# The first search of a token router: four rounds of 32 thresholds, or three rounds that begin with 128

## The chip, the cores and the metric

The kernel runs on one core of one Trainium2 chip. A core has five engines that work side by side, each through its own instructions in their order: TensorE (PE, matrix multiplies), VectorE (DVE), ScalarE (ACT), GpSimd (POOL) and SyncE (SP, which here only issues transfers). The metric is the device time of one execution in microseconds (us), lower is better. Before the change the median of three runs is 596.17 us (596.12 to 596.48).

## The reference

An attention block with pooled keys and values feeds a mixture of experts whose tokens are assigned greedily. What matters here is the assignment:

```python
def _moe_ref(x, w_gate, w1, w2):
    N, D = x.shape                      # 4608 tokens, 512
    E = w_gate.shape[1]                 # 8 experts
    cap = N // E                        # 576 places each
    logits = x @ w_gate
    order = np.argsort(-logits.flatten())
    assigned = -np.ones(N, dtype=np.int64)
    counts = np.zeros(E, dtype=np.int64)
    for idx in order:
        tok, e = (int(idx) // E, int(idx) % E)
        if assigned[tok] >= 0 or counts[e] >= cap:
            continue
        assigned[tok] = e
        counts[e] += 1
    out = np.zeros((N, D), dtype=np.float32)
    for e in range(E):
        mask = assigned == e
        h = np.maximum(x[mask] @ w1[e], 0.0)
        out[mask] = h @ w2[e]
```

Here x is the output of attention (8 batches, 8 heads, 576 positions, head size 64, keys and values averaged over groups of 8), seen as 4608 rows of 512.

## The kernel before

**Attention in 36 tiles.** The 4608 tokens are worked through in 36 tiles of 128, numbered 0 to 35; a tile is also a column of the routing arrays (128 partitions, 36 columns, 8 experts). The loop in `run` (class `Attention`) is a software pipeline. In its step n, TensorE computes the scores of tile n (`st_s`, L230, into the one PSUM buffer `pss`), then transposes the softmax of tile n-1 (`st_e`, L259) and multiplies tile n-2 with the values (`st_av`, L272). VectorE takes the row maximum of the scores (L240, `mx`) and subtracts it (L241, `e`), and then norms tile n-3 (`norm`: reciprocal L284, gate logits L287, and L297 `xt`). Every fourth tile, a reduction (L290, `lg`) writes the logits of four tiles; only the last four tiles do that one by one. Scores of tile n+1 cannot begin before `e` of tile n has emptied `pss`. Since an engine takes its instructions in order, whatever VectorE is given at the end of step n stands in front of the row maximum of tile n+1.

GpSimd sums the keys and values of the next batches over their groups of 8 (`pool_k` L175 to L179, `pool_v` L188 to L198), batch after batch; the last batch is finished in step 29. In two steps of each batch TensorE also prepares its values (`prep_v` L211, `prep_g` L220).

**The first search.** The greedy assignment is done expert by expert: the router looks for the logit value at which the first expert becomes full, gives all tokens above it to their best expert, closes that expert and goes on. The value is found by thresholds. Each token's best logit is turned into a place on a scale (`q`), compared with `J` = 32 levels (`cmp`), and TensorE counts, for each level and expert, the tokens above it, column by column: a matmul with `cmp` as weights and the one-hot best expert `oh` as moving operand (L709). A test finds the levels at which some expert has more than 576 (`over`, L751), a matmul of ones counts these levels and spreads the result to all partitions (L755), and the scale is made finer by 32/1.125 round the level found. This is done four times (`rounds` = 4) in `search_first`.

What can be done before the last logits are there is spread over the steps of attention, by the dictionary handed to `A.run` in the kernel's main function. Its keys are the tile that has just been normed, so key k is worked off at the end of step k+3: the range of all logits of the first 24 columns in three steps (`bounds`, keys 25 to 27), best logit, place and one-hot of columns 0 to 27 (`best`, key 28), comparison of columns 0 to 15 and 16 to 27 (keys 29, 30), the levels themselves (key 31) and finer places (key 32). The columns 28 to 33, 34 and 35 follow in `begin`, between the last pieces of attention in `finish`.

After the search, `close` builds the list of rows of the expert; its number goes to a load of expert weights, the list to GpSimd, which gathers the rows. In between, matmuls that only keep TensorE busy are run (`warm`, L530). Then the expert's matmuls begin (L1210), and the searches of the other experts run beside them.

## Time and profile before

| | |
|---|---|
| median of three runs | 596.17 us |
| the profiled execution's own time | 596.39 us |
| its span, first to last instruction | 594.6 us |
| PE busy, share of the span | 574.0 us, 97% |
| DVE busy | 392.9 us, 66% |
| ACT busy | 305.1 us, 51% |
| POOL busy | 178.6 us, 30% |
| chain that ended last, by engine | PE 83%, issue 7%, DVE 4%, POOL 3%, DMA 1% |

The time of an execution is a little longer than the span, since it includes what lies before the first and after the last instruction. The page divides the span into 40 slices of 14.9 us. TensorE is 90% busy or more in all of them but the first, the last and the one from 134 to 149 us, where it is 50% to 60% busy and its granted clock is 0.6 of full speed. That is the passage from attention to the experts.

### The profile page before, as it was taken

To read this page: it belongs to the slowest core of one execution; us is meant where nothing else is said; L and a number is where in the kernel's file an instruction comes from. 1 tells how busy PE (TensorE), PEld (TensorE's weight loads), DVE (VectorE), ACT (ScalarE), POOL (GpSimd) and SP (SyncE) were. 2 spreads that over 40 slices of the span, in tenths; PEclk is the share of its full clock that TensorE was granted. 3 is DMA by queue.
4 is the path that set the end of the run, shared out by engine and by line. 5 is a ranking of instruction groups with operands and counts; after the bars stand their busy time and mean duration, and the time that the engine had idled before them with its cause. 6 is when DMAs were issued, how large, how long until landed. Compare 5 with 4: busy or idle time off the path is not lost.

```text
span 594.6 us, 11103 instructions
## 1 busy us (share of the span) xinstructions
PE 574.0 (97%) x4061; PEld 509.3 (86%) x4061; DVE 392.9 (66%) x1146; ACT 305.1 (51%) x633; POOL 178.6 (30%) x228
## 2 busy tenths in 40 slices
PE   8999999995999999999999999999999999999993
PEld 5899999993898799779978987997899899889972
DVE  7677887998886788668866876586487346416200
ACT  6444444452551385376665575285549627835210
POOL 1999999200200410330122221112221212210021
PEclk9999999996999999999999999999999999999997
DMA  8999982112540863538438336543743553350010
GB/s 352 420 423 399 424 321 88 74 72 96 181 143 29 255 204 122 144 107 291 98 99 277 105 81 221 168 107 76 265 129 81 189 201 89 89 196 10 2 58 26
DMA packets 63872, 99.83 MB, mean 168 GB/s; under 512 B 34736, under 2 KB 34752, under 8 KB 61120
## 3 DMA queue, kind: packets, MB, share of 16 engines
q1 hardware_dynamic: 52560, 70.66, 34.8%
q0 software_dynamic: 5920, 18.89, 10.0%
q10 hardware_dynamic: 5328, 9.48, 4.3%
q8 instruction: 34, 0.56, 0.4%
q14 instruction: 30, 0.25, 0.1%
HBM read 72.40 MB, written 18.87 MB: 154 GB/s over the span
## 4 chain that ended last, share of the span: by engine, by line
PE 83%; issue 7%; DVE 4%; POOL 3%; DMA 1%; ACT 0%; POOLq 0%; another core or an unknown queue 0%; ACTq 0%; DVEq 0%
PE h L1210 32%; PE h L1246 27%; PE psa L272 6%; PE pss L230 5%; PE h L1251 4%; PE pse L259 2%; PE rt L259 1%; PE rt L530 1%; PE rt L657 1%; DVE e L241 1%; PE rt L220 1%; PE rt L709 1%; DMA out_dram<-yt,rows 1%; PE h L530 1%; PE tp L1183 1%
## 5 line engine op out<-in xcount | busy, mean ns | idle before, releaser
L1246 PE MATMUL h<-w2h,hh 128*128 128x512 f32 x256 | 102.0, 398 | 0.3 <-PEq L1327 0.3
L1246 PE MATMUL h<-w2h,hl 128*128 128x512 f32 x256 | 101.4, 396 | 0.0
L1246 PE MATMUL h<-w2l,hh 128*128 128x512 f32 x256 | 101.0, 395 | 0.0
L1226 POOL DMA_INDIRECT out_dram<-yt,rows x36 | 38.0, 1056 | 193.9 <-ACT yt L1266 167.8
L1215 ACT ACTIVATE hh<-h 128x256 fp32r<-128x256 f32 (+2 forms) x129 | 52.7, 409 | 83.6 <-PE h L1210 83.2
L1210 PE MATMUL h<-xh,w1h 128*128 128x256 f32 (+2 forms) x516 | 93.4, 299 | 0.2 <-ACT xh L1185 0.2
L1210 PE MATMUL h<-xl,w1h 128*128 128x256 f32 (+2 forms) x516 | 91.9, 298 | 0.0
L1210 PE MATMUL h<-xh,w1l 128*128 128x256 f32 (+2 forms) x516 | 90.6, 296 | 0.0
L1210 PEld LDWEIGHTS h<-xh,w1h 128*128 128x128 f32 x516 | 77.0, 190 | 1.2 <-ACT xh L1185 0.5
L1210 PEld LDWEIGHTS h<-xl,w1h 128*128 128x128 f32 x516 | 76.4, 190 | 0.1
L1210 PEld LDWEIGHTS h<-xh,w1l 128*128 128x128 f32 x516 | 76.1, 190 | 0.0
L1114 POOL DMA_INDIRECT xa<-xd,rows x33 | 33.6, 1017 | 137.0 <-ACT xg L1137 40.5
L1220 DVE SCALAR_TENSOR_TENSOR hl<-h,hh 128x256 fp32r<-128x256 f32 (+2 forms) x129 | 56.9, 448 | 21.5 <-ACT hl L1218 10.9
L1266 ACT ACTIVATE yt<-h 128x512 f32<-128x512 f32 x32 | 19.1, 596 | 92.1 <-PE h L1246 78.9
L272 PE MATMUL psa<-vblk,eT 128*128 128x146 f32 (+3 forms) x390 | 59.3, 302 | 0.1
L1246 PEld LDWEIGHTS h<-w2h,hh 128*128 128x128 f32 x256 | 48.3, 189 | 9.3 <-issue 0.7
L1246 PEld LDWEIGHTS h<-w2l,hh 128*128 128x128 f32 x256 | 48.2, 188 | 9.2
L1246 PEld LDWEIGHTS h<-w2h,hl 128*128 128x128 f32 x256 | 48.4, 189 | 8.4
L1163 DVE TENSOR_TENSOR w1l<-raw,w1h 128x512 fp32r<-128x512 f32 x64 | 41.9, 686 | 17.8 <-ACT w1h L1159 17.6
L272 PEld LDWEIGHTS psa<-vblk,eT 128*128 128x128 f32 (+1 forms) x390 | 50.8, 180 | 1.5 <-issue 0.3
L1172 DVE TENSOR_TENSOR w2l<-raw,w2h 128x512 fp32r<-128x512 f32 x64 | 43.3, 682 | 3.3 <-ACT w2h L1169 3.1
L230 PE MATMUL pss<-kblk,rawq 128*128 128x144 f32 (+1 forms) x320 | 43.6, 294 | 0.1
(256 smaller groups left out, 947.1 us busy)
## 6 DMA issues: line engine op xcount, KB each, us to landing
...
```

What stands on the lines that cost most here:

```text
L230: nc.tensor.matmul(ps[cols, j // 2, 144 * (j % 2):144 * (j % 2) + 144], self.q_of(b, j, n, cols.stop - cols.start), self.kblk[b % 4][:, j] ...
L272: self.nc.tensor.matmul(o[h], self.eT[i][:, c, h], self.vblk[b % 4][:, self.BLOCKS[c]:self.BLOCKS[c + 1]], start=(c == cs[0]), stop=(c == ...
L1114: self.nc.gpsimd.indirect_dma_start(out=to[:n], out_offset=None, in_=self.xd, in_offset=bass.IndirectOffsetOnAxis(ap=rows[:n, t:t + 1], ax ...
L1163: self.nc.vector.tensor_tensor(l, raw, h.bitcast(F32), op=OP.subtract)
L1172: self.nc.vector.tensor_tensor(self.w2l[:, i], self.raw2[e][:, i], self.w2h[:, i].bitcast(F32), op=OP.subtract)
L1210: nc.tensor.matmul(ps[:, :m], a[:, j, fs], b[:, j, o], start=(n == 0), stop=(n == 11))
L1215: nc.scalar.activation(hh[:, f, o], ps[:, :m], AF.Relu)
L1220: later(0.65, 0.4, lambda f=f, o=o, m=m, ps=ps: nc.vector.scalar_tensor_tensor(hl[:, f, o], ps[:, :m], 0.0, hh[:, f, o].bitcast(F32), op0= ...
L1226: st = nc.gpsimd.indirect_dma_start(out=rows, out_offset=bass.IndirectOffsetOnAxis(ap=idx, axis=0), in_=y, in_offset=None)
L1246: nc.tensor.matmul(ps, a[:, f, o], b[:, f], start=(f == 0 and k == 0), stop=(f == 7 and k == 2))
L1251: nc.tensor.matmul(ps, self.hl[:, f, 512:], b[:, f], start=(f == 0 and k == 0), stop=(f == 7 and k == 1))
L1266: self.nc.scalar.activation(y, ps, AF.Copy)
```

## The change

The first search does three rounds. The first round has 128 levels, one for each row of the counting matmul's output; the two others have 32 as before. The scale of the first round spans the best logits of the first 16 columns and not all logits of 24. The range is found in seven small steps (`range_of`), on VectorE at keys 16, 17, 18, 21 and 22, with two matmuls that stand in steps 21 and 24 straight behind the scores (`mid`) and whose results ScalarE copies out of PSUM. The comparisons of the first round write 128 levels a column into a buffer of the pool of query tiles (`room`), six columns a step at keys 24 to 27. The last four columns compare logits with levels in 32-bit numbers (`late_tiles`). The product of one-hot and expert weight (`wish`) is done in two parts. The core of the diff (the tiles `thr`, `gz` and `ow` move to a pool that ends with attention; `best`, `top` and the code that is only renamed are left out):

```diff
+            for f in mid.get(n, ()):
+                f()
             e = [lambda g=g: self.st_e(n - 1, g) for g in range(2 if n >= 1 else 0)]
...
-    def bounds(self, wk, cols):
...
+    def range_of(self, i, n=16):
+        nc, wk = self.nc, self.wk
+        lg = self.lg[:, :n].rearrange("p c e -> p (c e)")
+        if i == 0:
...
+            nc.vector.tensor_reduce(self.mm[:, 0:1], lg, axis=AX.X, op=OP.max)
+            nc.vector.tensor_reduce(self.mm[:, 1:2], lg, axis=AX.X, op=OP.min)
+        elif i == 1:
+            nc.vector.tensor_reduce(self.bv[:, :n], self.lg[:, :n], axis=AX.X, op=OP.max)
+            nc.vector.tensor_reduce(self.mm[:, 2:3], self.bv[:, :n], axis=AX.X, op=OP.min)
+            nc.vector.tensor_scalar(self.mm[:, 1:3], self.mm[:, 1:3], -1.0, None, op0=OP.mult)
+        elif i == 2:
+            ps = self.psum()
+            nc.tensor.transpose(ps[:3, :128], self.mm, self.ident)
+            self.m3 = wk.tile([3, 128], F32, name="m3")
+            nc.scalar.activation(self.m3, ps[:3, :128], AF.Copy)
+        elif i == 3:
+            m = wk.tile([3, 1], F32, name="m1")
+            nc.vector.tensor_reduce(m, self.m3, axis=AX.X, op=OP.max)
+            self.d3 = wk.tile([3, 3], F32, name="d3")
+            nc.vector.tensor_scalar(self.d3, self.ident[:3, :3], m, None, op0=OP.mult)
...
+        elif i == 4:
+            ps = self.psum()
+            nc.tensor.matmul(ps[:, :3], self.one3, self.d3, start=True, stop=True)
...
+        elif i == 5:
+            b = self.b
+            nc.vector.tensor_scalar(b[:, 3:5], b[:, 1:3], b[:, 0:1], None, op0=OP.add)
+            nc.vector.scalar_tensor_tensor(self.lo0, b[:, 3:4], -0.125, b[:, 1:2], op0=OP.mult, op1=OP.subtract)
...
+            nc.vector.scalar_tensor_tensor(self.lo1, b[:, 4:5], -0.125, b[:, 2:3], op0=OP.mult, op1=OP.subtract)
+        elif i == 6:
...
+            nc.vector.tensor_scalar(self.steps1, self.shares[:, :3], w, None, op0=OP.mult)
...
+            nc.vector.scalar_tensor_tensor(self.los, self.steps1[:, 0:1], -1.0 - EDGE, self.lo1, op0=OP.mult, op1=OP.add)
...
+    def fresh(self, c0, c1, n=0):
+        nc = self.nc
+        if c1 > n:
+            c = max(c0, n)
+            nc.vector.tensor_reduce(self.bv[:, c:c1], self.lg[:, c:c1], axis=AX.X, op=OP.max)
+        bv = self.bv[:, c0:c1]
+        nc.vector.tensor_scalar(self.q2[:, c0:c1], bv[:, :, None].to_broadcast([128, c1 - c0, 2]), self.lo1, self.scale1,
+                                op0=OP.subtract, op1=OP.mult)
+        nc.vector.tensor_tensor(self.oh[:, c0:c1], self.lg[:, c0:c1], bv[:, :, None].to_broadcast([128, c1 - c0, 8]),
+                                op=OP.is_equal)
+
+    def compare(self, c0, c1):
+        n = c1 - c0
+        if c0 == 0:
+            self.cmp0 = self.room()
+        self.nc.vector.tensor_tensor(self.cmp0[:, c0:c1].rearrange("p c (j t) -> p c j t", t=2),
+                                     self.q2[:, c0:c1, None].to_broadcast([128, n, 64, 2]),
+                                     self.jrow[:, None].to_broadcast([128, n, 128]).rearrange("p c (j t) -> p c j t", t=2),
+                                     op=OP.is_gt)
+
+    def late_tiles(self, c0, c1):
+        nc, n = self.nc, c1 - c0
+        bv = self.bv[:, c0:c1]
+        nc.vector.tensor_reduce(bv, self.lg[:, c0:c1], axis=AX.X, op=OP.max)
+        nc.vector.tensor_tensor(self.cmp0[:, c0:c1], self.thr[:, None].to_broadcast([128, n, 128]),
+                                bv[:, :, None].to_broadcast([128, n, 128]), op=OP.is_lt)
...
-        for k in range(rounds):
-            last = k + 1 == rounds
...
+        ps = self.psum()
+        count(0, NC - 1, lambda c: self.cmp0[:, c])
+        yield 0
+        up = self.bank("pse")[:, :1]
+        self.place(NC - 12, NC)
+        count(NC - 1, NC, lambda c: self.cmp0[:, c])
+        test(0, self.gz)
+        nc.tensor.matmul(up, self.ones, self.gz, start=True, stop=True)
+        for k in (1, 2):
+            q2 = wk.tile([128, NC, 2], F16, name="q2")
+            finer(q2, self.q32[:, :, None].to_broadcast([128, NC, 2]))
+            compare(0, 4, 12, 24, NC)
...
     def begin(self, g):
-        self.best(self.NC - 8, self.NC - 2)
+        NC = self.NC
+        self.compare(NC - 8, NC - 4)
+        self.late_tiles(NC - 4, NC - 2)
+        yield
+        self.late_tiles(NC - 2, NC - 1)
         next(g)
         yield
...
+        A.run(c2, R, lambda: R.consts(A.jp, A.ident), R.more, {
+            16: f(R.range_of, 0), 17: f(R.range_of, 1), 18: f(R.range_of, 3), 20: f(R.before_search, 1),
+            21: f(R.range_of, 5), 22: f(R.range_of, 6) + f(R.before_search, 0), 23: f(R.fresh, 0, 24, 16),
+            24: f(R.compare, 0, 6), 25: f(R.compare, 6, 12), 26: f(R.compare, 12, 18), 27: f(R.compare, 18, 24),
+            28: f(R.fresh, 24, 28), 29: f(R.compare, 24, 28) + f(R.levels), 30: f(R.place, 0, 24) + f(R.wish, 0, 24)
+            + f(wake, nc, R, rwk, moe_w2), 31: f(R.fresh, 28, 32)}, {21: f(R.range_of, 2), 24: f(R.range_of, 4)},
```

Where that puts the instructions, at three places. Line numbers are those of each kernel's own file. First, VectorE in step 26 of attention, before: the subtraction for tile 26, the norm of tile 23 with the reduction of four tiles, and the maximum of tile 27.

```order
L241 TENSOR_TENSOR e<-pss,mx 128x576
L284 RECIPROCAL rinv<-psa 128x8
L287 TENSOR_TENSOR gt_1206<-psa,rinv 128x64
L290 TENSOR_REDUCE lg<-gt_1206 128x32
L297 TENSOR_TENSOR xt<-psa,rinv 128x512
L240 TENSOR_REDUCE mx<-pss 128x8
L241 TENSOR_TENSOR e<-pss,mx 128x576
```

And in the change, from the last instruction of step 25 (`los`, the lowest level) to the maximum of tile 27 (`bv` is the best logit, `q2a` the places, `oh` the one-hot):

```order
L594 SCALAR_TENSOR_TENSOR los<-steps_1325,lo_1290 128x1
L245 TENSOR_REDUCE mx<-pss 128x8
L246 TENSOR_TENSOR e<-pss,mx 128x576
L289 RECIPROCAL rinv<-psa 128x8
L292 TENSOR_TENSOR gt_1224<-psa,rinv 128x64
L295 TENSOR_REDUCE lg<-gt_1224 128x32
L302 TENSOR_TENSOR xt<-psa,rinv 128x512
L617 TENSOR_REDUCE bv_264<-lg 128x8
L619 TENSOR_SCALAR q2a<-bv_264,lo_1290,scale_1327 128x48
L621 TENSOR_TENSOR oh_266<-lg,bv_264 128x192
L245 TENSOR_REDUCE mx<-pss 128x8
```

Three instructions now stand between the norm of tile 23 and the maximum of tile 27. Second, TensorE in step 21, before: scores of tile 21, transposes of tile 20, values of tile 19.

```order
L230 MATMUL pss<-kblk_130,rawq 128x144 x4
L259 MATMUL pse<-ident,e 127x128 x3
L272 MATMUL psa<-vblk_177,eT_172 128x2x73
L272 MATMUL psa<-vblk_177,eT_172 128x3x73
L272 MATMUL psa<-vblk_177,eT_172 128x2x73
```

And in the change (`mm` holds the maximum and the two minima of each partition, written at the end of step 20 by VectorE):

```order
L235 MATMUL pss<-kblk_130,rawq 128x144 x4
L563 MATMUL rt<-ident,mm 3x128
L264 MATMUL pse<-ident,e 127x128 x3
L277 MATMUL psa<-vblk_177,eT_172 128x2x73
L277 MATMUL psa<-vblk_177,eT_172 128x3x73
```

The transpose of `mm` stands in front of the transposes of tile 20. Third, VectorE at the end of attention, from the norm of tile 32 to the reciprocal of tile 34, before:

```order
L297 TENSOR_TENSOR xt<-psa,rinv 128x512
L575 TENSOR_SCALAR q_1681<-bv_262,lo_260,scale 128x28
L284 RECIPROCAL rinv<-psa 128x8
L287 TENSOR_TENSOR gt_1700<-psa,rinv 128x64
L290 TENSOR_REDUCE lg<-gt_1700 128x8
L594 TENSOR_REDUCE bv_262<-lg 128x6
L597 TENSOR_SCALAR q2a<-bv_262,lo_260,scale 128x12
L601 TENSOR_TENSOR oh_264<-lg,bv_262 128x48
L702 TENSOR_TENSOR cmp<-q2a,jrow 128x192
L284 RECIPROCAL rinv<-pss 128x8
```

And in the change (`rawq` is the buffer that holds the comparisons of the first round):

```order
L302 TENSOR_TENSOR xt<-psa,rinv 128x512
L289 RECIPROCAL rinv<-psa 128x8
L292 TENSOR_TENSOR gt_1720<-psa,rinv 128x64
L295 TENSOR_REDUCE lg<-gt_1720 128x8
L629 TENSOR_TENSOR rawq<-q2a,jrow 128x512
L638 TENSOR_REDUCE bv_264<-lg 128x2
L639 TENSOR_TENSOR rawq<-thr,bv_264 128x256
L641 TENSOR_TENSOR oh_266<-lg,bv_264 128x16
L289 RECIPROCAL rinv<-pss 128x8
```

One instruction has gone from behind the norm, and the four of `begin` are others and longer.

## Rows read from the trace of the kernel before

**Rows 1.** The view of stretches for the passage between attention and the experts: stretch and length, then busy time and number of instructions of PE, PEld (TensorE's weight loads), DVE, ACT and POOL, then granted TensorE clock, DMA share and GB/s.

```profile
135.00:143.00 8.00, 4.62 (x115) 3.68 (x114) 6.51 (x36) 2.94 (x13) 0.30 (x4) 0.66 0.20 72
143.00:152.00 9.00, 5.80 (x29) 2.56 (x29) 6.69 (x24) 2.41 (x5) 3.19 (x4) 0.54 0.58 175
```

**Rows 2.** The timeline of the first search from the second round on: start, duration, engine, line, operation, and in brackets idle time before it with what ended it. The tests of the second, third and fourth round, the list of rows, and the first matmul of the first expert.

```profile
137.37 0.17 DVE L751 TENSOR_SCALAR_CACHE_REDUCE over<-rt 32x8 bf16<-32x8 f32 x1
...
139.70 0.17 DVE L751 TENSOR_SCALAR_CACHE_REDUCE over<-rt 32x8 bf16<-32x8 f32 x1
...
142.03 0.17 DVE L751 TENSOR_SCALAR_CACHE_REDUCE over<-rt 32x8 bf16<-32x8 f32 x1
...
147.45 0.17 DVE L850 TENSOR_SCALAR rows<-found 128x5 int32<-128x5 int16 x1
...
152.55 0.67 PE L1210 MATMUL h<-xh,w1h 128*128 128x128 f32 x4 [0.25 <-ACT xh L1185]
```

**Rows 3.** The timeline of VectorE in attention: the row maxima of tiles 21, 24, 25 and 27 with the engine's idle time before them in brackets, the subtraction for tile 27, and the instruction that precedes the maximum of tile 28.

```profile
80.37 0.76 DVE L240 TENSOR_REDUCE mx<-pss 128x8 f32<-128x576 f32 x1 [0.43 <-PE pss L230]
...
90.54 0.76 DVE L240 TENSOR_REDUCE mx<-pss 128x8 f32<-128x576 f32 x1 [0.28 <-PE pss L230]
...
93.80 0.76 DVE L240 TENSOR_REDUCE mx<-pss 128x8 f32<-128x576 f32 x1 [0.67 <-PE pss L230]
...
99.99 0.75 DVE L240 TENSOR_REDUCE mx<-pss 128x8 f32<-128x576 f32 x1
100.84 0.76 DVE L241 TENSOR_TENSOR e<-pss,mx 128x576 f32<-128x576 f32 x1
...
103.77 0.25 DVE L221 TENSOR_TENSOR vblk<-rt,mask 128x88 f32<-128x88 f32 x1 [1.20 <-PE rt L220]
```

**Rows 4.** The timeline of TensorE: the start of the scores of tiles 20, 24, 29 and 33.

```profile
76.07 1.25 PE L230 MATMUL pss<-kblk,rawq 128*128 128x144 f32 x8
...
89.26 1.25 PE L230 MATMUL pss<-kblk,rawq 128*128 128x144 f32 x8
...
105.60 1.25 PE L230 MATMUL pss<-kblk,rawq 128*128 128x144 f32 x8
...
119.88 1.25 PE L230 MATMUL pss<-kblk,rawq 128*128 128x144 f32 x8
```

**Rows 5.** The timeline of TensorE's weight loads: the transposes of tile 20 in step 21, the scores of tile 28, and the small 32-bit matmul of the range before.

```profile
80.05 0.42 PEld L259 LDWEIGHTS pse<-ident,e 128*127 128x127 f32 x3
...
101.89 1.05 PEld L230 LDWEIGHTS pss<-kblk,rawq 128*128 128x128 f32 x8
...
112.01 0.29 PEld L557 LDWEIGHTS rt<-d,one 2*128 2x128 f32 x2 [0.25 <-ACT eT L260]
```

**Rows 6.** The timeline of VectorE in the range's first step before: a reduction and the instruction that reads its result.

```profile
106.69 0.34 DVE L544 TENSOR_REDUCE mm<-lg 128x1 f32<-128x192 f32 x1
107.07 0.15 DVE L545 TENSOR_SCALAR mm<-mm 128x1 f32<-128x1 f32 x1
```

**Rows 7.** The view of instructions by line and shape on VectorE from 60 to 145 us: line, operation, names, shapes and count, then busy us, mean ns of one, and idle time before.

```profile
L702 DVE TENSOR_TENSOR cmp<-q2a,jrow 128x512 bf16<-128x512 f16 x1 | 0.4, 416 | 0.0
L601 DVE TENSOR_TENSOR oh<-lg,bv 128x224 bf16<-128x224 f32 x1 | 0.4, 384 | 0.0
L583 DVE TENSOR_TENSOR cmp<-thr,bv 128x32 bf16<-128x32 f32 x2 | 0.4, 191 | 0.1
...
L702 DVE TENSOR_TENSOR cmp<-q2a,jrow 128x384 bf16<-128x384 f16 x1 | 0.3, 348 | 0.0
```

**Rows 8.** The timeline of VectorE at the end of attention: the levels at key 31 and the maximum of tile 35 behind them, the places at key 32, the first instruction of `begin`, and the reciprocal of tile 34.

```profile
127.58 0.29 DVE L568 TENSOR_SCALAR thr<-i,steps,lo 128x32 f32<-128x32 f32 x1
127.79 0.75 DVE L240 TENSOR_REDUCE mx<-pss 128x8 f32<-128x576 f32 x1
...
130.59 0.29 DVE L575 TENSOR_SCALAR q<-bv,lo,scale 128x28 f32<-128x28 f32 x1
...
131.59 0.20 DVE L594 TENSOR_REDUCE bv<-lg 128x6 f32<-128x48 f32 x1
...
132.33 0.20 DVE L284 RECIPROCAL rinv<-pss 128x8 f32<-128x8 f32 x1
```

**Rows 9.** The timeline of GpSimd over the last batch: x2 and x3 are instructions in a row, with their summed time.

```profile
93.93 2.64 POOL L175 TENSOR_TENSOR tk<-rawk 128x1152 f32<-128x1152 f32 x1
96.64 1.41 POOL L176 TENSOR_TENSOR tk<-tk 128x576 f32<-128x576 f32 x1
98.13 1.65 POOL L179 TENSOR_TENSOR kblk<-tk 64x288 f32<-64x288 f32 x2
99.85 2.90 POOL L188 TENSOR_TENSOR t<-rawv 128x1280 f32<-128x1280 f32 x1
102.83 1.53 POOL L189 TENSOR_TENSOR t<-t 128x640 f32<-128x640 f32 x1
104.44 0.86 POOL L190 TENSOR_TENSOR vsum<-t 128x320 f32<-128x320 f32 x1
105.39 1.65 POOL L198 TENSOR_TENSOR vblk<-vsum,mask 128x128 f32<-128x128 f32 x3
```

**Rows 10.** The timeline of the kernel's first microseconds: a VectorE instruction on the 128x128 array of indices `jp`, a GpSimd memset that runs beside it, and a VectorE instruction on the same array later, with GpSimd idle.

```profile
1.13 0.78 DVE L66 TENSOR_SCALAR ident<-jp 128x128 f32<-128x128 int32 x1 [1.13 <-POOL jp L64]
...
1.26 0.57 POOL L76 MEMSET kblk<- 128x576 f32 x1
...
7.97 0.23 DVE L476 TENSOR_SCALAR tri<-jp 128x128 bf16<-128x128 int32 x1
```

More of the change, by code (lines that the diff above doesn't have):

```diff
@@ L332, in bank, with run @@
         return self.ps.tile(shape, F32, name=name, bufs=bufs)
-    def run(self, ctx, full, consts, more, after, end, warm):
+    def run(self, ctx, R, consts, more, after, mid, end, warm):
         tc, nc = self.tc, self.nc
@@ L367, in first_k @@
             self.pool_k(0, nc.vector, (kh[0], slice(2, 3)))
-        self.local(ctx.enter_context(tc.tile_pool(name="loc", bufs=1)), full, consts, more, first_k)
+        self.local(ctx.enter_context(tc.tile_pool(name="loc", bufs=1)), R.ones, consts, more, first_k)
         for b in range(1, B):
@@ L515, in before_search @@
             nc.vector.memset(self.cmp[:, :3], 0.0)
+            nc.vector.tensor_scalar(self.jrow, self.jp, self.pcol, None, op0=OP.add)
         else:
@@ L566, in levels @@
     def levels(self):
[L568 to L569 removed]
+        self.nc.vector.tensor_scalar(self.thr, self.jrow, self.steps1[:, 0:1], self.lo1, op0=OP.mult, op1=OP.add)
     def place(self, c0, c1):
@@ L652, in search @@
             if k == 3:
-                self.top(lo)
+                self.top(steps[:, 3:4], lo)
             yield 1.25, 1.9
@@ L686, in search, with top, search_first @@
         nc.vector.tensor_scalar(self.sel, q16, up, 1.0 + EDGE, op0=OP.subtract, op1=OP.is_gt)
[L688 removed]
+    def top(self, step, lo):
         self.hi = self.wk.tile([128, 1], F32, name="hi")
[L690 to L697 removed]
+        self.nc.vector.scalar_tensor_tensor(self.hi, step, self.J + 2.0, lo, op0=OP.mult, op1=OP.add)
+    def search_first(self):
+        nc, wk, NC, J, steps = self.nc, self.wk, self.NC, self.J, self.steps1
+        cmp, lo = self.cmp, self.los
         def compare(*cuts):
@@ L930, in phase @@
         else:
-            yield from self.search(sh) if k else self.search_first(sh)
+            yield from self.search(sh) if k else self.search_first()
         if k == 0:
@@ L1306 @@
     NC = N // 128
-    R.bank = A.bank
+    R.bank, R.room = A.bank, A.room
     with ExitStack() as c2:
         g = R.run()
-        bounds = R.bounds(rwk, NC - 12)
-        step = lambda: next(bounds, None)
-        start = lambda: next(g)
-        A.run(c2, R.ones, lambda: R.consts(A.jp, A.ident), R.more, {NC - 16: [lambda: R.before_search(1)], NC - 14: [lambda: R.before_search(0)], NC - 11: [step], NC - 10: [step], NC - 9: [step], NC - 8: [lambda: R.best(0, NC - 8)],
-                                                       NC - 7: [start], NC - 6: [start, lambda: wake(nc, R, rwk, moe_w2)],
-                                                       NC - 5: [R.levels], NC - 4: [lambda: R.place(0, NC - 8)]},
+        f = lambda f, *a: [lambda: f(*a)]
+        A.run(c2, R, lambda: R.consts(A.jp, A.ident), R.more, {
[4 more added lines that the diff above has]
+            + f(wake, nc, R, rwk, moe_w2), 31: f(R.fresh, 28, 32)}, {21: f(R.range_of, 2), 24: f(R.range_of, 4)},
               R.begin(g), R.warm)
```

159 lines of the change are left out of this document (60 added, 99 removed).

## The prediction

> **What bounds the kernel now.** I read the page's slices first: TensorE is 90% busy or more everywhere but at both ends and in one slice around 140 us. The view of stretches shows this passage: from 135 to 143 us TensorE is busy 4.62 of 8.00 us, from 143 to 152 us 5.80 of 9.00, at a granted clock of 0.66 and 0.54, which is time at the lower of its two levels, 1.2 GHz [rows 1]. Here the first search sets the end: VectorE and TensorE hand each other one round after the other, then follow the list of rows at 147.45 and the first matmul of the first expert at 152.55 [rows 2]. All that comes later waits for this list and for the number of the expert, so a microsecond gained or lost before it moves the end by as much. Then the timeline of attention in front of it: TensorE looks full there, but its scores wait for VectorE's subtraction. The idle time of VectorE before a row maximum is the reserve for added work: 0.43 us in an ordinary tile, 0.28 and 0.67 in two others, nothing before tile 27, 1.20 before the instruction that precedes the maximum of tile 28 [rows 3]. What an added instruction takes beyond this reserve delays the maximum, the subtraction and the next scores.
>
> **The round that goes.** The tests of the rounds stand at 137.37, 139.70 and 142.03: a round takes 2.33 us, all of it on the chain [rows 2]. One middle round goes, whole: -2.33.
>
> **Steps 28 to 32 of attention.** From the scores of tile 20 to those of tile 24 it is 13.19 us, from tile 29 to tile 33 it is 14.28 [rows 4], though the pattern of batches is the same nine tiles later. The 1.09 us between them are what the old range and the old `best` cost there, two small matmuls with their waits among it. In the change these steps carry a comparison of 768 elements, or three small instructions. 512 elements take 0.416 us, 384 take 0.348 [rows 7], which is 0.53 ns an element and 0.55 us for 768. Of that some 0.08 overlap with the next instruction, so the 0.43 of an ordinary tile just covers it. If that cover is a tenth short, three tiles cost 0.3. I take a gain of 1.0, between 0.7 and 1.1.
>
> **Steps 16 to 27.** They had no routing work but memsets. Steps 16 to 19 of the loop stay as they are, and what key 16 adds in step 19 (two reductions, 0.4) the reserve covers.
> - Step 20: reduction of 128 elements, about 0.28 (48 take 0.20 [rows 8], 192 take 0.34 [rows 6]), reduction of 16 (0.17), negation (0.15), each reading the one before and so starting 0.04 after its end [rows 6]. The engine is free from 79.94, 0.43 before the maximum at 80.37 [rows 3]; so `mm` is written at about 80.5. TensorE would begin the transposes of tile 20 at 80.05 [rows 5], and in front of them now stands the transpose of `mm`. It waits 0.5 us, with it the transposes of tile 20, the values of tile 19 and the scores of tile 22, and behind those VectorE. +0.55 with the transpose itself; between 0.3, if VectorE is earlier, and 0.7.
> - Step 24: the small 32-bit matmul behind the scores. Its like took 0.29 us of weight loads [rows 5]: +0.3, at least 0.1 for the issue alone. ScalarE's two copies lie in its own idle time (it is busy 51% of the span): nothing.
> - Step 25: four small instructions, about 0.65 against a reserve of 0.43: +0.15, between 0 and 0.25.
> - Step 26: best logit (64 elements, 0.22), places (about 0.2 until the next can start) and one-hot (192 elements; 224 take 0.384 [rows 7]), 0.75 in all, in front of a maximum that had no reserve at 99.99. The subtraction of tile 27 ended at 101.60 (100.84 and 0.76 [rows 3]), and the scores of tile 28 began at 101.89 [rows 5], so 0.2 is covered: +0.55, between 0.3 and 0.75.
> - Step 27: the first comparison, 0.55, has the 1.20 of reserve [rows 3]: nothing. The other instructions of steps 21 to 23 fit into 0.4 each.
>
> **The end of attention.** From 127.58 on VectorE has no idle time left [rows 8], so every instruction counts. Key 31: three instructions of 0.5 together for the levels, which held up the maximum by 0.21 (127.58 to 127.79): +0.3. Key 32: the places of 0.29 are gone, 0.2 of it on the path: -0.2. `begin`: 131.59 to 132.33 is 0.74 before; now a comparison of 512 (0.416) that need not wait for the last logits, two small instructions, and a 32-bit comparison of 256. 32 elements take 0.191, 224 take 0.384 of the same 32-bit kind [rows 7], so 1.0 ns an element and 0.42 for 256; in a row about 0.9: +0.15. Tiles 34 and 35: 128 for 32 elements, +0.1 each. The second part of `wish` before the test of the middle round: +0.05. Sum +0.5, between 0.2 and 0.9.
>
> Without anything else: -2.33 - 1.0 + 0.55 + 0.3 + 0.15 + 0.55 + 0.5 = -1.3.
>
> **What the trace of before does not show: VectorE beside GpSimd.** From 15 to 107 us GpSimd adds keys and values almost without a gap, in instructions of 0.55 to 2.90 us [rows 9]. In all that time VectorE reads its large operand from PSUM (scores, sums) or runs a reduction; only the memsets of key 20 and one 128x1 negation at 107.07 [rows 6] are otherwise. The change puts into steps 20 to 28 instructions whose inputs all lie in SBUF: negation (20), `d3` (21), `jrow` (23), three at key 21 (step 24), two at key 22 (step 25), places and one-hot (26), comparisons (27, 28). One place shows such a pair: the very first VectorE instruction, 128x128 from SBUF to SBUF, took 0.78 us where its like took 0.23 with GpSimd idle, and it ended at 1.91, 0.08 after GpSimd's memset ended at 1.83 [rows 10]. I read it as held until GpSimd let go. Against this speaks that it is the engine's first instruction, which may cost more by itself.
>
> A request at a random moment finds, of GpSimd's instruction, the sum of squares over twice the sum left: durations of 2.64, 1.41, 2x0.82, 2.90, 1.53, 0.86 and 3x0.55 [rows 9] give 22.7 / 25.3 = 0.9 us. Bounds: nothing at the one end (rows 10 as a first instruction). If only instructions with two SBUF inputs wait, once in each of steps 24 to 27 (in step 28 GpSimd is done by then): 3.6, less reserves of 0.3 in step 24 and 0.7 in step 27: 2.6. If all kinds wait, another three (steps 20, 21, 23), less 0.4 of reserve: 4.9. If each step's second request waits again, for GpSimd takes its turn in between, 2.7 more: about 7.6. A gain I exclude, since nothing gets shorter by it. I take 3.8: the 2.6 whole and half of what the small ones would add.
>
> The one row that has such a pair shows 0.78 against 0.23 us [rows 10]. The Trainium skill (SBUF — State Buffer, section "SBUF: two separate sides") says that VectorE and GpSimd share one pair of SBUF ports as an exclusive lock held for a whole instruction, when VectorE's instruction has two SBUF inputs or runs in a two-port mode. By that rule the waits are those of all kinds, 4.9, and the time some 599.8 us; by the row as a first instruction's cost it would be 594.9. The trace agrees with the rule for a one-input instruction beside a memset; for two inputs no run here shows it.
>
> **Sum.** -1.3 + 3.8 = +2.5 on the profiled execution's own 596.39 (its span of 594.6 and 1.8 around it): 598.9. The median of the runs shown is 0.2 below that execution: forecast 598.7 us, slower; its own range 597.3 to 603.
>
> **Rivals.**
> - *No waits behind GpSimd.* The sum of -1.3 alone, 596.39 - 1.3 - 0.2: 594.9 (594.1 to 595.7). For it: rows 10 is one row, and of the engine's first instruction. Against it: the end at 1.91 fits the memset too well.
> - *The added work is hidden as well*, because the steps of attention have more room than I give them and the transpose of `mm` does not wait: -2.33 and about what else the end costs, less a part of the gain of steps 28 to 32: 593.8. Against it: no idle time before the maximum of tile 27 [rows 3].
> - *The clock.* Granted clock is at the lower level through the passage [rows 1] and must rise before the first expert. If the first 3 us of its matmuls still ran at half speed, 1.5 us would be lost, on top of the rival without waits: 596.4, no change. Against it: nothing changes in the warm matmuls that stand in front of the expert.
> - *The change does not do what it says*: 16 columns give too narrow or 128 levels too coarse a scale, and the slow path behind the flag runs all experts again, 594.6 - 152.55 = 442 us more. Nothing in the profile speaks for it.
>
> **Chances.** Forecast 0.50, no waits 0.33, all hidden 0.10, clock 0.05, others 0.02. A measurement of this kernel can tell about 0.2%, 1.2 us, from no change. The case without waits lies just at that border: 0.20 of its 0.33 faster, 0.13 the same. Faster 0.30, same 0.20 (with the clock and a little of the forecast), slower 0.50. The range from 594.3 to 601.5 leaves out about a tenth on each side.
>
> **What would show it.** Right: beside GpSimd, VectorE's `oh` of step 26, the comparisons of steps 27 and 28, `los` and `jrow` last or stand much longer than 0.4 us and end with a GpSimd instruction; scores of tile 29 begin 3 us or more later than 105.60; a wait of half a microsecond before the transpose of `mm`; three tests 2.3 us apart. Wrong: comparisons of 0.55 us beside running GpSimd instructions, and scores of tile 33 at about 120 us. Then the first rival holds.

## The result and the profile after

The changed kernel takes 601.37 us (median of six runs) beside 596.36 us for the kernel before on the same chip: the medians are 5.0 us apart. The ratio of the means is 1.0093, 95% interval 1.0083 to 1.0103; one of the six runs, at 604.42 us, raises it a little. The change is slower. Forecast were 598.7 us. The direction was right; the rise of 2.5 is half of what was measured.

Where the 5 us are is read from TensorE's timeline: the scores of tiles 20, 24, 26, 27, 29 and 33 after the change.

```profile
75.87 1.25 PE L235 MATMUL pss<-kblk,rawq 128*128 128x144 f32 x8
...
90.09 1.18 PE L235 MATMUL pss<-kblk,rawq 128*128 128x144 f32 x8
...
99.51 1.22 PE L235 MATMUL pss<-kblk,rawq 128*128 128x144 f32 x8 [2.54 <-DVE rinv L289]
105.92 1.22 PE L235 MATMUL pss<-kblk,rawq 128*128 128x144 f32 x8 [3.26 <-DVE rinv L289]
...
113.30 1.25 PE L235 MATMUL pss<-kblk,rawq 128*128 128x144 f32 x8
...
126.60 1.25 PE L235 MATMUL pss<-kblk,rawq 128*128 128x144 f32 x8
```

From tile 20 to tile 29 it is now 37.43 us; before it was 29.53 [rows 4]. Two brackets, 2.54 and 3.26, hold most of the difference: TensorE stands still before tiles 26 and 27. The reciprocal named there is the one that ended last by the profile; it takes 0.20 us and is not the cause. What VectorE did in steps 24 and 25 shows it (VectorE's timeline, then GpSimd's):

```profile
93.82 2.61 DVE L581 TENSOR_SCALAR b<-b 128x2 f32<-128x2 f32 x1
96.46 0.16 DVE L582 SCALAR_TENSOR_TENSOR lo<-b 128x1 f32<-128x1 f32 x1
96.54 1.37 DVE L584 SCALAR_TENSOR_TENSOR lo<-b 128x1 f32<-128x1 f32 x1
...
100.25 0.15 DVE L588 TENSOR_SCALAR width<-b 128x1 f32<-128x1 f32 x1
100.43 2.17 DVE L590 TENSOR_SCALAR steps<-shares,width 128x3 f32<-128x3 f32 x1
102.63 0.16 DVE L592 RECIPROCAL scale<-steps 128x1 f32<-128x1 f32 x1
102.72 1.49 DVE L594 SCALAR_TENSOR_TENSOR los<-steps,lo 128x1 f32<-128x1 f32 x1
```

```profile
93.78 2.63 POOL L175 TENSOR_TENSOR tk<-rawk 128x1152 f32<-128x1152 f32 x1
96.48 1.41 POOL L176 TENSOR_TENSOR tk<-tk 128x576 f32<-128x576 f32 x1
...
99.68 2.90 POOL L188 TENSOR_TENSOR t<-rawv 128x1280 f32<-128x1280 f32 x1
102.66 1.53 POOL L189 TENSOR_TENSOR t<-t 128x640 f32<-128x640 f32 x1
```

Read them side by side. `b` works on 256 numbers, lasts 2.61 and ends at 96.43, 0.02 after GpSimd's 2.63 (96.41). The second instruction gets in before GpSimd's next one; the third is again held, to 97.91, when the 1.41 ends (97.89). In step 25 the same: `steps` ends at 102.60 (GpSimd 102.58), `los` at 104.21 (104.19). GpSimd's instructions keep their durations [rows 9]. In step 25 stands `width`, one column, 0.15 us beside a running 2.90: not held.

The end of the passage, VectorE's timeline of the three tests and of the list of rows:

```profile
142.22 0.17 DVE L772 TENSOR_SCALAR_CACHE_REDUCE over<-rt 128x8 bf16<-128x8 f32 x1
...
144.57 0.17 DVE L772 TENSOR_SCALAR_CACHE_REDUCE over<-rt 32x8 bf16<-32x8 f32 x1
...
146.89 0.17 DVE L772 TENSOR_SCALAR_CACHE_REDUCE over<-rt 32x8 bf16<-32x8 f32 x1
...
152.31 0.17 DVE L892 TENSOR_SCALAR rows<-found 128x5 int32<-128x5 int16 x1
```

Three tests, 2.35 and 2.32 apart; the list 4.86 later than in [rows 2]. The first test of the kernel before, which [rows 2] does not have, was

```profile
135.09 0.17 DVE L751 TENSOR_SCALAR_CACHE_REDUCE over<-rt 32x8 bf16<-32x8 f32 x1
```

To tell apart where a kernel loses, this table takes the scores of tiles 20, 24, 29 and 33 and the last test of the first search from each trace (us between them; names as in the experiments below):

| kernel | 20 to 24 | 24 to 29 | 29 to 33 | 33 to last test | sum, against before |
|---|---|---|---|---|---|
| before | 13.19 | 16.34 | 14.28 | 22.15 | 65.96 |
| after | 14.22 | 23.21 | 13.30 | 20.29 | 71.02, +5.06 |
| no_sums | 14.20 | 17.18 | 13.31 | 20.30 | 64.99, -0.97 |
| one_column | 13.75 | 18.45 | 13.31 | 20.29 | 65.80, -0.16 |
| only_24 | 14.20 | 18.07 | 13.30 | 20.50 | 66.07, +0.11 |
| transpose_later | 15.30 | 23.20 | 13.31 | 20.29 | 72.10, +6.14 |
| spread | 14.10 | 17.19 | 13.43 | 20.03 | 64.75, -1.21 |
| spread2 | 13.64 | 16.84 | 13.70 | 20.11 | 64.29, -1.67 |

The loss is all in the first two columns; in the last two the change wins 0.98 and 1.86.

### The profile page after: what moved, and what is told of

Read it like the earlier page. It is cut to its first block, busy times and chain, and to the rows that moved or that the text cites. A ratio compares the mean times of both kernels' runs of the same rounds, so it can differ in the third digit from the quotient of the medians.

```text
span 599.6 us, 11035 instructions
## 1 busy us (share of the span) xinstructions
PE 572.0 (95%) x4024; PEld 507.8 (85%) x4024; DVE 402.2 (67%) x1150; ACT 306.3 (51%) x634; POOL 179.0 (30%) x228
## 4 chain that ended last, share of the span: by engine, by line
PE 79%; DVE 7%; issue 7%; DMA 4%; SPq 1%; POOL 1%; another core or an unknown queue 0%; POOLq 0%; ACT 0%; DVEq 0%; ACTq 0%
PE h L1253 32%; PE h L1289 26%; PE psa L277 5%; PE pss L235 5%; PE h L1294 4%; DMA rawq<-in_q_dram 3%; PE pse L264 1%; DVE e L246 1%; PE rt L707 1%; PE rt L264 1%; DVE mx L245 1%; DVE xt L302 1%; PE rt L220 1%; DMA out_dram<-yt,rows 1%; PE h L539 1%
## 5 line engine op out<-in xcount | busy, mean ns | idle before, releaser
L235 PEld LDWEIGHTS pss<-kblk,rawq 128*128 128x128 f32 (+1 forms) x320 | 37.2, 179 | 10.7 <-issue 5.0
```

Of the source, the lines that this page charges most:

```text
L235: nc.tensor.matmul(ps[cols, j // 2, 144 * (j % 2):144 * (j % 2) + 144], self.q_of(b, j, n, cols.stop - cols.start), self.kblk[b % 4][:, j] ...
```

## The experiments

Each group ran beside the kernel before on its own chip, where that took 596.85 to 597.54 us; ratios are against it.

**1. one_column.** Theory: VectorE's instructions wait behind GpSimd's. Rival: the added instructions cost the time themselves.

```diff
-            nc.vector.tensor_scalar(b[:, 3:5], b[:, 1:3], b[:, 0:1], None, op0=OP.add)
-            nc.vector.scalar_tensor_tensor(self.lo0, b[:, 3:4], -0.125, b[:, 1:2], op0=OP.mult, op1=OP.subtract)
+            for c in (1, 2):
+                nc.vector.tensor_scalar(b[:, c + 2:c + 3], b[:, c:c + 1], b[:, 0:1], None, op0=OP.add)
+            nc.vector.tensor_scalar(self.lo0, b[:, 3:4], -0.125, b[:, 1:2], op0=OP.mult, op1=OP.subtract)
...
-            nc.vector.tensor_scalar(self.steps1, self.shares[:, :3], w, None, op0=OP.mult)
+            for c in range(3):
+                nc.vector.tensor_scalar(self.steps1[:, c:c + 1], self.shares[:, c:c + 1], w, None, op0=OP.mult)
```

> The changed kernel, its range written with instructions of one column and one SBUF input each (seven more small instructions than in the change; the steps and what is computed stay). In the changed kernel's trace the one-column form (width, 0.15 us beside a running GpSimd instruction) was the only small one that was not held. Theory 'waits behind GpSimd': the five stretched instructions of steps 24 and 25 (2.61, 1.37, 2.17, 1.49) and of steps 20 and 21 (0.57, 1.37) last 0.15 to 0.2 each and end with no GpSimd instruction; VectorE is then not past GpSimd's end, so that the one-hot of step 26 and the first comparison of step 27, with two SBUF inputs, are held instead, for 1.5 to 3 together: 597 us (596 to 598.5). Rival 'the added instructions themselves, their chain of results': more instructions in the same chain, 601.4 to 602.

Measured: 597.18 us, ratio 1.0003 (0.9993 to 1.0012). The edits of `mm`, `d3`, `lo1` and `los` are of the same kind and left out here. Six more instructions in all (1156 on VectorE for 1150; the expectation counts seven), and nearly all of the 5 us gone, as the theory has it. VectorE's timeline of steps 24 to 26:

```profile
93.48 0.33 DVE L584 TENSOR_SCALAR b<-b 128x1 f32<-128x1 f32 x2
...
97.18 0.46 DVE L594 TENSOR_SCALAR steps<-shares,width 128x1 f32<-128x1 f32 x3
...
101.08 1.41 DVE L623 TENSOR_SCALAR q2a<-bv,lo,scale 128x48 f16<-128x48 f32 x1
102.41 0.35 DVE L625 TENSOR_TENSOR oh<-lg,bv 128x192 bf16<-128x192 f32 x1
```

What was 2.61 is two instructions of 0.33 together. One wait of more than 1 us remains, in step 26, and it is the places that are held (0.31 in the changed kernel, where GpSimd's sums were done), not the one-hot; that got in behind them.

**2. no_sums.** GpSimd's sums of the last two batches are left out (but for one instruction of 0.86 each), VectorE's work is untouched.

```diff
         src = self.rk.pop(b)
+        if b > 5:
+            return
...
+        if b > 5:
+            eng.tensor_tensor(self.sums[b], src[:, :, :64], src[:, :, 64:128], op=OP.add)
+            return
```

> The changed kernel without GpSimd's sums of keys and values for the last two batches (each keeps one instruction of 0.86 us for values, so the results of these batches are other ones, and this part of the work is left out). GpSimd is then idle beside steps 20 to 28, VectorE's instructions are those of the change. Theory 'waits behind GpSimd': all small instructions at 0.15 to 0.35 us, scores of tile 29 at about 106, no more than 0.8 later than 105.60, end of the kernel at 594.9 (594.3 to 595.7), what the prediction's sum gives without waits. Rival 'the added instructions themselves': scores of tile 29 at 113, 600.9 to 601.9 us.

Measured: 596.24 us, ratio 0.9981 (0.9970 to 0.9993). The same instructions as in the change, with GpSimd idle in steps 24 and 25:

```profile
93.94 0.22 DVE L586 TENSOR_SCALAR b<-b 128x2 f32<-128x2 f32 x1
94.20 0.16 DVE L587 SCALAR_TENSOR_TENSOR lo<-b 128x1 f32<-128x1 f32 x1
94.27 0.15 DVE L589 SCALAR_TENSOR_TENSOR lo<-b 128x1 f32<-128x1 f32 x1
...
97.81 0.23 DVE L595 TENSOR_SCALAR steps<-shares,width 128x3 f32<-128x3 f32 x1
```

And `mm` in step 20, then TensorE's scores of tiles 20 and 29:

```profile
80.32 0.59 DVE L565 TENSOR_SCALAR mm<-mm 128x2 f32<-128x2 f32 x1
...
76.01 1.25 PE L240 MATMUL pss<-kblk,rawq 128*128 128x144 f32 x8
...
107.39 1.25 PE L240 MATMUL pss<-kblk,rawq 128*128 128x144 f32 x8
```

So the stretch needs GpSimd, and the rival falls. The expected start of tile 29 was missed: from tile 20 to tile 29 it is 31.38, 1.85 more than before and not 0.8. I had not carried the prediction's own terms for steps 20 to 26 (1.55) into that number. With them it fits to 0.3, and 37.43 - 31.38 = 6.05 is what the waits that this kernel lacks cost in the changed one. One wait it still has: GpSimd's sums of the batch before run until 80.89, and `mm` in step 20 lasts 0.59, where `b`, of the same form, takes 0.22. From tile 21 to tile 22 it is 4.13 here, 3.68 in one_column, where `mm` is not held, and 3.07 before. So some 0.4 of the 31.38 (an estimate from these two) is a wait too. The end is 0.8 us lower than before by the medians and 1.1 by the ratio; 1.3 was expected.

**3. probe.** Which forms are held: the kernel before, one useless instruction to a key (`y` and `x` are small SBUF tiles).

```diff
+        if i == 2:
+            v.tensor_scalar(y[:, :1], x[:, :1], 2.0, None, op0=OP.mult)
...
+        elif i in (7, 21):
+            v.scalar_tensor_tensor(y[:, :1], x[:, :1], 2.0, self.shares[:, :1], op0=OP.mult, op1=OP.add)
...
+        elif i == 10:
+            v.tensor_scalar(self.pj, self.jp, self.pcol, None, op0=OP.add)
```

> The kernel before, with small VectorE instructions of no use in keys 2 to 19 and 21, one form to a key, beside a running GpSimd, to see which forms are held. Theory 'waits behind GpSimd' in the narrow form (two SBUF inputs only): tensor_tensor and scalar_tensor_tensor stretch to the end of a GpSimd instruction, tensor_scalar of any width, reciprocal and reduction last 0.15 to 0.25. In the wide form (any instruction with more than one 32-bit column from SBUF as well, from the changed kernel's 128x2 and 128x3): the tensor_scalar of 2 and 3 columns are held too, the one of 1 column and the one that reads integers are not. Two dependent instructions of a held form take two GpSimd instructions, eight of one column take 8 x 0.15. Rival 'the stretch has to do with the chain, not with GpSimd': none is stretched, since none waits for a result of the same key except in two keys. Time: 0.5 us or so for each held one beyond the reserve, 600 to 606 us; if none is held 596 to 597.

Measured: 603.76 us, a single run. VectorE's timeline, and two of GpSimd's instructions:

```profile
28.84 0.14 DVE L550 TENSOR_SCALAR py<-px 128x1 f32<-128x1 f32 x1
...
36.79 0.40 DVE L554 TENSOR_SCALAR py<-px 128x3 f32<-128x3 f32 x1
...
42.95 1.13 DVE L558 TENSOR_TENSOR py<-px,shares 128x1 f32<-128x1 f32 x1
47.58 2.70 DVE L560 SCALAR_TENSOR_TENSOR py<-px,shares 128x1 f32<-128x1 f32 x1
...
60.45 2.98 DVE L566 TENSOR_SCALAR pj<-jp,pcol 128x128 f16<-128x128 int32 x1
...
82.85 0.48 DVE L576 TENSOR_SCALAR py<-px 128x2 f32<-128x2 f32 x1
83.36 0.17 DVE L577 TENSOR_SCALAR px<-py 128x2 f32<-128x2 f32 x1
```

```profile
47.36 2.90 POOL L188 TENSOR_TENSOR t<-rawv 128x1280 f32<-128x1280 f32 x1
...
60.44 2.90 POOL L188 TENSOR_TENSOR t<-rawv 128x1280 f32<-128x1280 f32 x1
```

One number per partition from two SBUF inputs took 2.70, to the end of a 2.90. The wide theory holds for `tensor_scalar` of two and three columns, and one expectation of it fell: the one that reads integers is held too (2.98, where the like of it took 0.23 [rows 10]). Eight of one column in a row took 0.14 to 0.15 each; a reciprocal of two columns (0.15) and a reduction (0.15), each beside a running GpSimd instruction, were not held either. Two dependent held ones did not take two GpSimd instructions: the second began 0.03 after the first, in the gap before GpSimd's next.

**4. transpose_later.** Does an earlier gain survive the waits?

```diff
-18: f(R.range_of, 3)
+19: f(R.range_of, 3)
...
-{21: f(R.range_of, 2), 24: f(R.range_of, 4)}
+{22: f(R.range_of, 2), 24: f(R.range_of, 4)}
```

> The changed kernel with the transpose of mm and the step behind it (m, d3) one tile later, step 22 instead of 21, so that TensorE does not wait for mm. Theory 'waits behind GpSimd': the held instructions of steps 24 and 25 end when GpSimd's instructions end, at 96.43, 97.9, 102.6 and 104.2, however early they stand there; the 0.5 to 0.9 us won at step 21 are lost again at step 24: 601.2 us (600.9 to 601.6). Rival 'each term adds up on its own': 0.55 less, 600.8, or 0.9 less, 600.5.

Measured: 603.33 us, ratio 1.0096 (1.0079 to 1.0113); neither number. On this chip the kernel before takes 597.06, 0.7 more than beside the changed kernel, so the theory's number moves to some 602 (an estimate). One of the four runs took 602.08, the other three 603.27 to 603.55.

Tile 22 starts 0.69 earlier against tile 20 than in the changed kernel (6.46 for 7.15 us), but by tile 24 that is more than lost: 15.30 for 14.22. The transpose of `mm` now waits 0.58 us for a ScalarE copy, and `d3` in step 22 lasts 2.25 and ends with GpSimd's 2.90. Tile 27 all the same starts 0.10 earlier than in the changed kernel (29.95 for 30.05): the waits of steps 24 and 25 end by GpSimd's clock, and what stood before them, here 1.08 us more, does not count. Then something else comes, in the view of stretches of this kernel and then of after_again, the changed kernel once more (columns as in [rows 1]):

```profile
106.00:108.00 2.00, 1.98 (x11) 1.99 (x12) 1.93 (x6) 0.54 (x1) 1.84 (x3) 0.67 0.00 0
108.00:110.00 2.00, 2.00 (x10) 1.94 (x9) 1.86 (x6) 0.98 (x2) 0.19 (x1) 0.50 0.38 135
```

```profile
106.00:108.00 2.00, 1.69 (x7) 1.72 (x8) 1.90 (x7) 0.68 (x1) 1.84 (x3) 0.50 0.00 0
108.00:110.00 2.00, 2.00 (x13) 1.99 (x12) 1.70 (x4) 0.71 (x2) 0.48 (x1) 0.65 0.39 135
```

The granted clock goes to the lower level about where the pause of 3.26 ends, and from tile 27 to tile 28 it is 4.97 us. The edit is not the reason: in after_again the clock falls at the same place and these tiles are 4.81 us apart, while the first trace of the same kernel has 3.69 and a clock of 1.00 there. What decides no run here tells. Between transpose_later and after_again the stretch from tile 20 to the last test differs by 0.08 us (72.10 and 72.02), so nothing of the earlier gain is left there.

**5. after_again and only_24.** Has each held step its own price, or that of the moment?

> The changed kernel once more, beside the kernels of this group, as their reference: 4.9 to 5.3 us above the kernel before.

Measured: 601.93 us, ratio 1.0080 (1.0065 to 1.0095); the medians are 5.1 us apart.

> The changed kernel with only step 24 written in one-column forms (b, lo0, lo1); step 25 keeps its three-column steps and its los with two SBUF inputs, step 26 its places. In the changed kernel the scores of the next tile came 2.6 late at step 24 and 3.3 late at step 25. Theory 'a held instruction waits for the end of whatever GpSimd instruction runs, so its price is not its own but that of the moment': with step 24 free, VectorE stands in step 25 at 97.2 instead of 100.4, beside the end of the 1.41 and the two 0.8 instead of the 2.90; steps and los are held 0.5 and 0.8 together some 1.3, and the places of step 26 at 101.8 by the 2.90 for 0.6; scores of tile 28 at 105.0 (104.3 to 105.8), the end 4.2 us (3.5 to 5) below the changed kernel. Rival 'each held step has its own price': 2.6 below the changed kernel, the 3.3 of step 25 stay.

Measured: 597.05 us, ratio 1.0002 (0.9993 to 1.0012): 4.9 below the changed kernel (expected 4.2, rival 2.6), by changing step 24 alone. VectorE's timeline of steps 25 and 26:

```profile
98.36 0.23 DVE L591 TENSOR_SCALAR steps<-shares,width 128x3 f32<-128x3 f32 x1
98.62 0.17 DVE L593 RECIPROCAL scale<-steps 128x1 f32<-128x1 f32 x1
98.70 0.73 DVE L595 SCALAR_TENSOR_TENSOR los<-steps,lo 128x1 f32<-128x1 f32 x1
...
102.69 0.60 DVE L620 TENSOR_SCALAR q2a<-bv,lo,scale 128x48 f16<-128x48 f32 x1
```

`steps`, 2.17 in the changed kernel, is 0.23 here, since VectorE came at the end of the 1.41 instead of in the 2.90. A held instruction has no price of its own.

**6. dose_wide and dose_one.** The wait by itself, in the kernel before.

```diff
+        v.tensor_scalar(y[:, :2], x[:, :2], self.pcol, None, op0=OP.add)
+        v.scalar_tensor_tensor(z[:, :1], y[:, :1], -0.125, x[:, :1], op0=OP.mult, op1=OP.subtract)
+        v.scalar_tensor_tensor(z[:, 1:2], y[:, 1:2], -0.125, x[:, 1:2], op0=OP.mult, op1=OP.subtract)
```

> The kernel before with three instructions of no use at key 21 (step 24), in the forms of the change: one of two columns and, behind it, two of one column with two SBUF inputs. It measures the wait by itself: nothing of the change is there. VectorE is free there at 93.1 and has 0.67 to the maximum at 93.80 [rows 3]; GpSimd's three short instructions end at 93.93, its 2.64 runs from 93.93 to 96.57 [rows 9]. Theory 'waits behind GpSimd': the first is held to the end of one of the short ones, the second gets into the gap, the third is held to 96.57 and the maximum behind it stands there too: 2.8 us late (2 to 3), and as nothing later in this kernel is held, the end is 2.8 later than before (1.8 to 3.2). Rival 'the added instructions': 0.55 of work under 0.67 of reserve, no change (0 to 0.3).

> The same place, inputs and results as in the kernel with the three instructions, in one-column forms (four instructions, 0.15 to 0.2 each). Both theories: 0.65 of work under 0.67 of reserve, no change (0 to 0.3); were it 1 or more, the forms would not be what decides.

Measured: dose_wide 600.68 us, ratio 1.0059 (1.0043 to 1.0074); dose_one 598.28 us, 1.0014 (1.0005 to 1.0024). Three small instructions against four: 2.4 us. VectorE's timeline of dose_wide:

```profile
93.97 0.55 DVE L543 TENSOR_SCALAR py<-px,pcol 128x2 f32<-128x2 f32 x1
94.55 2.55 DVE L544 SCALAR_TENSOR_TENSOR pz<-py,px 128x1 f32<-128x1 f32 x1
97.03 0.15 DVE L545 SCALAR_TENSOR_TENSOR pz<-py,px 128x1 f32<-128x1 f32 x1
```

And GpSimd's:

```profile
92.84 1.65 POOL L198 TENSOR_TENSOR vblk<-vsum,mask 128x128 f32<-128x128 f32 x3
94.45 2.63 POOL L175 TENSOR_TENSOR tk<-rawk 128x1152 f32<-128x1152 f32 x1
97.17 1.40 POOL L176 TENSOR_TENSOR tk<-tk 128x576 f32<-128x576 f32 x1
```

It was the second that was held by the 2.63, and the third that got into the gap, the other way round than expected; the sum is nearly the same. Here GpSimd's 2.63 begins at 94.45, 0.04 before the instruction ahead of it ends (94.49), so the first held one finds no gap behind it. The next GpSimd instruction begins 0.08 after the 2.63 has ended, and there the third gets in. dose_one came out 0.8 above before, expected were 0 to 0.3. Its trace shows no loss at this place (tile 25 to 26 3.05 us, before 3.06), but 0.34 between tiles 23 and 24, a step ahead of the dose, and in dose_wide likewise. There VectorE's subtraction for tile 23 waits 0.46 us for a ScalarE copy, which it does not in the kernel before. Why is open.

**7. spread, spread2, spread3.** Versions in which nothing, or little, is held. In `spread` ScalarE makes `d3` and the places, the rest has one column:

```diff
-        nc.vector.tensor_scalar(self.q2[:, c0:c1], bv[:, :, None].to_broadcast([128, c1 - c0, 2]), self.lo1, self.scale1,
-                                op0=OP.subtract, op1=OP.mult)
+        nc.scalar.activation(self.q2[:, c0:c1], bv[:, :, None].to_broadcast([128, c1 - c0, 2]), AF.Identity, bias=self.nb,
+                             scale=self.scale1)
...
-24: f(R.compare, 0, 6)
+24: f(R.hot, 0, 24) + f(R.compare, 0, 6)
```

> The change with nothing that is held in steps 20 to 26: one-column forms; ScalarE makes d3 and the places q2 (one ACTIVATE with a factor and an offset of one column each); the transpose of mm one tile later; the one-hot of tiles 0 to 23 in step 27 in front of the first comparison; the other shares, los and lo0 after GpSimd's end. What is computed stays. Theory 'waits behind GpSimd': against the one-column kernel the 1.1 of the held places, 0.3 of the one-hot in step 26, 0.3 of step 25, 0.3 of TensorE's wait for mm go, and 0 to 0.6 comes in step 27, where one-hot and comparison can be held by GpSimd's last instructions of 0.86 and 0.55: 1.4 below it, 1.3 below the kernel before (0.6 to 2). Rival 'the one-column kernel was only better placed in GpSimd's time or clock': no gain against it, equal to the kernel before.

Measured: 595.77 us, ratio 0.9979 (0.9970 to 0.9988), 1.1 (medians) to 1.3 (ratio) below before, as expected. In `spread2` three steps move once more:

```diff
-24: f(R.hot, 0, 24) + f(R.compare, 0, 6), 25: f(R.compare, 6, 12)
+24: f(R.compare, 0, 6), 25: f(R.hot, 0, 24) + f(R.compare, 6, 12)
...
-30: f(R.place, 0, 24) + f(R.wish, 0, 24)
+30: f(R.place, 0, 24, nc.gpsimd) + f(R.wish, 0, 24, nc.gpsimd)
...
-19: f(R.range_of, 3)
+18: f(R.range_of, 2), 19: f(R.range_of, 3)
...
-{22: f(R.range_of, 2), 24: f(R.range_of, 4)}
+{24: f(R.range_of, 4)}
```

> The kernel 'spread' with three steps put elsewhere: the transpose of mm at the end of step 21, behind the values of tile 19, so that it does not wait for the shared PSUM buffer behind ScalarE (0.7 of wait in step 22 of 'spread'); the one-hot of tiles 0 to 23 in step 28, after GpSimd's end, instead of step 27 (where it took 0.70 and pushed the comparison behind a GpSimd instruction); places and wish of tiles 0 to 23 on GpSimd, which is idle there. Theory 'what is left in spread are these two waits': 0.6 and 0.3 less, 0.1 for key 30: 0.8 us below 'spread' (0.3 to 1.2), 1.9 below the kernel before. Rival 'the steps have no more room': equal to 'spread', 1.1 below the kernel before.

> The kernel 'spread2' once more, beside the next one: 1.2 to 2.2 below the kernel before.

Measured: 595.83 us, ratio 0.9970 (0.9959 to 0.9980), and again 595.19 us, 0.9969 (0.9957 to 0.9981): 1.8 us below the kernel before, the fastest here. Against `spread` that is 0.5 us by the ratios, whose intervals overlap; 0.8 was expected. `spread3` makes `jrow` on ScalarE:

> The kernel 'spread2' with jrow (128x128, integers in, 16 bits out) made by ScalarE instead of VectorE. In 'spread2' this instruction of step 23 lasted 0.87 and ended with a GpSimd instruction, and from the scores of tile 24 to those of tile 25 it was 3.70, 3.25 in the kernel before. Theory 'waits behind GpSimd': 3.25 again, 0.45 less at the end (0.2 to 0.6). Rival 'ScalarE's instruction or the step itself delays as much': 3.6 to 3.7, no difference.

Measured: 595.68 us, ratio 0.9978 (0.9969 to 0.9987), no gain: from tile 24 to tile 25 it stays at 3.74. So moving `jrow` does not give the 0.45 back. What else the change puts into that step is the small 32-bit matmul, which the prediction has at 0.3. TensorE's timeline of no_sums, where `jrow` is not held (0.23), has most of it: the transposes begin 1.43 us after the scores of tile 24, before it was 1.08. The end is 0.5 later than in spread2_again for another reason, in VectorE's timeline:

```profile
137.01 0.26 DVE L778 TENSOR_SCALAR q<-q,pse 128x72 f16<-128x72 f32 x1 [0.68 <-POOL xt L331]
```

The second round waits for a GpSimd memset, which itself waits for a transfer. That this comes of having put the places on GpSimd is not shown: spread2_again has them there as well and no such wait.

## Why the prediction was half right

- **The round that goes, -2.33.** Right: the tests stand 2.35 and 2.32 apart, and from the scores of tile 33 to the last test it is 20.29 instead of 22.15, 1.86 less. That is -2.33 with **the end of attention** at +0.47, predicted +0.5. Most of this +0.47 stands ahead of the first test, which came 15.21 after the scores of tile 33 and now comes 15.62 after them.
- **Steps 28 to 32, -1.0.** Right: 14.28 became 13.30. (Its cover was a little short on paper: 0.55 less 0.08 is 0.47, for 0.43 of idle time.)
- **Steps 20 to 26 without waits, +1.55** (0.55, 0.3, 0.15, 0.55). Right in the sum: 1.85 in no_sums, or some 1.45 without the wait that `mm` has there. Term by term, from the starts of the scores in no_sums against before: +1.06 ahead of tile 22 (0.4 of it the wait of `mm`), +0.45 ahead of tile 25, -0.18 ahead of tile 27, where step 25's +0.15 should have stood, and +0.52 ahead of tile 28. In step 27 the reserve hid the comparison but for 0.1.
- **VectorE beside GpSimd, +3.8.** Here the sum went wrong: the waits cost 6.05, and with that of `mm` some 6.45. The reading of [rows 10] was right; the size was not, nor the places. The prediction let each of steps 24 to 27 wait once. In the changed kernel places, one-hot and comparisons of steps 26 and 27 were not held at all, because VectorE had by then slid past the end of GpSimd's sums at 106.86. The 6.05 fell into steps 24 and 25. (In step 21 `d3` was held too, 1.37 us, but from tile 20 to tile 24 the changed kernel is only 0.02 longer than no_sums.) The failing step is "a request at a random moment finds 0.9 us", once to a step. Steps 24 and 25 had two held instructions each, 2.61, 1.37, 2.17 and 1.49, together 7.64, or some 6.9 more than their own 0.15 to 0.2. The prediction has 0.9 for the first of each step and nothing for the second. The first ones waited some 4.3 together: `b` came 0.04 after GpSimd's 2.63 had begun, `steps` 0.75 after the 2.90 had. The second ones waited some 2.6, and theirs are not random moments: in both steps, when GpSimd's instruction ends, one VectorE instruction gets through, and the next but one meets GpSimd's new instruction at its start and waits for the whole. The moment of `steps` was not random either: VectorE had just been let go at 97.91, at the end of a GpSimd instruction, and came back 2.5 later; in only_24, without that wait, `steps` did not wait. That `b` met the 2.63 at its very start no experiment explains; it did so in after_again as well (94.24, GpSimd's instruction from 94.17). The prediction had second requests in its upper bound (7.6, "each step's second request waits again") and gave them no share of the 3.8; its own range, to 603, took that bound in and so holds the 601.37.
- **Sum.** +1.85 + 6.05 - 0.98 - 1.86 = 5.06, less the 0.20 by which tile 20 started earlier: the last test 4.86 later. With the 0.4 of `mm` among the waits, the forecast's -1.3 without waits becomes about -1.4.
- The Trainium skill (SBUF — State Buffer, section "SBUF: two separate sides") has the pair of ports as an exclusive lock, for whole instructions. The traces agree: 2.70 of waiting beside 2.90. It names two SBUF inputs or a two-port mode of VectorE; the runs show the first directly, and for a `tensor_scalar` with one input that several columns are held and one column is not. The mode itself no trace shows.
- **The rivals.** "No waits" was wrong for this kernel, though its 594.9 is near what no_sums (-1.1 us) shows. The clock was back before the first expert (1.00 from 156 us on, its first matmul at 157.43), as said; but the pause between tiles 26 and 27 brought a fall of the clock that no rival had, in after_again and not in the first trace.

## What to carry to other kernels

Beside GpSimd's sums, the form of a small VectorE instruction decides its time more than its size: one column from two inputs took 2.70 us, one column from one input and a factor 0.15 us. When small steps are spread over a stretch in which GpSimd works, write them with one column and one SBUF input, or give them to ScalarE, and price each of the others at a whole GpSimd instruction rather than half of one. A gain in front of such a wait may be worth nothing, since the wait ends when GpSimd's instruction does, and taking away the first wait may free the ones behind it.

## What had not been expected

- Behind a held instruction the next one gets into GpSimd's gap of 0.07 to 0.08 us, and the third does not. Where GpSimd leaves no gap, as at 94.45 in dose_wide, the second is held.
- VectorE holds GpSimd as well: in spread2_again a comparison that ended at 105.25 beside GpSimd made its instruction of 0.86 take 1.06; in only_24 one from 105.97 to 106.52 stands beside 0.80 for an instruction that takes 0.40 elsewhere.
- A pause of some 3.26 us of TensorE was followed by a granted clock of 0.50 in transpose_later and in after_again, where tiles 27 and 28 are 1.28 and 1.12 us further apart than in the first trace of the changed kernel; there the same pause left the clock at 1.00.
